# New waits, a reach for PSUM tiles, new due times and other batches in a list scheduler of a kernel of attention and two expert layers

## The chip, the cores and the metric

The kernel runs on one core of one Trainium2 chip. The metric is the device time of one execution in microseconds (us). The core's engines each work through their own list of instructions: TensorE (PE; PEld is its weight load), VectorE (DVE), ScalarE (ACT), GpSimd (POOL) and SyncE (SP), which issues the transfers.

## The reference

Attention keeps the 32 largest scores of each row (4 batches of 8 heads, 576 rows, 64 columns a head), and two gated layers follow it on 2304 rows of 512:

```python
scores = scale * np.matmul(q, k.transpose(0, 1, 3, 2))
kth = np.partition(scores, -top_k, axis=-1)[..., -top_k:-top_k + 1]
scores = np.where(scores >= kth, scores, -1e9)
attn = softmax(scores)                      # exp, divided by its sum
x = np.matmul(attn, v)                      # heads side by side: 2304 x 512
# layer 1
xn = x / np.sqrt(np.mean(x * x, -1) + 1e-6) * rms_g
g = xn @ w_gate
x = (g / (1 + np.exp(-g)) * (xn @ w_val)) @ w_out        # 512 -> 1536 -> 512
# layer 2
out = 1 / (1 + np.exp(-(x @ w_gate2))) * (x @ w_val2) @ w_out2
```

## The kernel before

The 2304 rows are 18 units of 128. For each unit VectorE takes the top 32 of eight tiles of scores (128 rows x 576, one head each): MAX8 finds eight, MATCH_REPLACE8 takes them out, four times over, and one product applies the threshold. The transposed probabilities (ph to pt, by a DMA transpose) are then multiplied by the values into pv, and the unit's rows x go into layer 1: `enter1` scales and transposes them into xt, `gate1` (gate and value product of 48 matmuls each, three times, for the three blocks of 512 columns) and `out1` (144 matmuls) make yt, and layer 2 does the same with `gate2` and `out2`. All operands are split into two float16 halves, so that each product is three.

The weights come as 64-bit numbers. `prep_piece` decodes one piece of 512 x 512 (load to raw, three steps on VectorE through a PSUM tile "dec", a matmul for the size, a scale, two float16 halves). Layer 1's nine pieces (`prep1`) stay in SBUF. Layer 2's nine pieces (`prep2`) are written to DRAM, and each batch of units loads all of them again (`load2`, 512 KB at a time) into a ring of seven buffers that raw and the halves being made use too. The first batch's loads come after the last piece (`AHEAD`, in `load2`).

Nothing is issued as it is written. A recorder (`record`, line 156) notes every operation with its engine, a planned duration (`cost`, line 185) and a due time `prio` that the program sets: TAU = 56 for a unit of attention, 7 for a tile, and for the layers a running `pos` plus a lag (line 959). The work of the layers is listed in stages (lines 946 to 962): in stage b the second layer of batch b-1 and the first layer of batch b alternate in proportion. VectorE's operations of the layers are due 160 earlier (`BIAS`).

`order` (line 212) then plays the program through. For each engine it looks at the operations whose inputs are recorded as done and whose buffers are free, takes the one that leaves the engine idle least, then the one due first; of the engines it takes the one that starts first. An operation's users may start at the time `done`, its end plus a latency by engine (260 ns for PE, 170 for VectorE, 200 for ScalarE, 150 for GpSimd) plus `MARGIN`, 120 ns. What comes out is the order of each engine's instructions and of each ring's buffers; the times on the chip follow from that order and from semaphores.

PSUM has two tiles for scores, one for pv, and three for all the rest (`ps_m`: pg, pw, py, po, dec, the small sums).

Of the kernel before, what the change touches and what calls it, by code (L numbers as in the profile page):

```python
# [16 lines left out]
PSUM = bass.MemoryType.PSUM  # L17
# [17 lines left out]
MARGIN = 120  # L35

TAU = 56.0
PREP1 = (-0.5, 0.1)  # L40
PREP2 = (0.8, 0.02)
LOADS = 0.9
LAG = (80, 1, 160)
BIAS = {"vector": 160}


BATCHES = (2,) * 9
AHEAD = 8


# [60 lines left out]


class _Op:
    __slots__ = "eng calls cost lat prio deps users waits tiles start end idx new later".split()


class _Engine:
# [7 lines left out]
class Scheduler:  # L125
# [30 lines left out]
    def record(self, eng, method, args, kw):  # L156
        writes = [x for x in (*args[:1], kw.get("out"), kw.get("accum_out")) if isinstance(x, _View)]
        reads = [x for x in (*args[1:], *(v for n, v in kw.items() if n not in ("out", "accum_out"))) if isinstance(x, _View)]
        new = not self.open
        if new:  # L160
            op = _Op()
            op.idx, op.eng, op.prio, op.calls, op.cost, op.deps, op.tiles = len(self.ops), eng, self.prio - self.bias.get(eng, 0.0), [], 0.0, set(), set()
            op.lat = 0.0
            self.ops.append(op)
            if self.open is not None:
                self.open.append(op)
        else:
            op = self.open[0]
        if self.first:
            op.deps.add(self.first)  # L170
            self.first = None
        op.calls.append((method, args, kw))
        cost, op.lat = self.cost(eng, method, args, kw, writes, reads)
        op.cost += cost
        for views, wr in ((reads, False), (writes, True)):
            for x in views:
                for other, o, w in x.tile.uses:
                    if (wr or w) and o is not op and x.overlaps(other):
                        op.deps.add(o)
        for views, wr in ((reads, False), (writes, True)):  # L180
            for x in views:
                x.tile.uses.append((x, op, wr))
                op.tiles.add(x.tile)

    def cost(self, eng, method, args, kw, writes, reads):

        out = (writes or reads)[0].shadow
        src = max([x.shadow for x in reads] + [out], key=lambda a: math.prod(a.shape[1:]))
        n = math.prod(src.shape[1:])
        psum = any(x.tile.pool.space == PSUM for x in reads + writes)  # L190
        ptrs = sum(isinstance(x, _View) for x in (*args[2:], kw.get("scalar"), kw.get("scale"), kw.get("bias")))
        if eng == "tensor":
            return math.prod(out.shape[1:]) / 2.4 + 1, 260
        if eng == "vector":
            if method in ("max", "match_replace", "tensor_tensor"):
                ptrs = 0
            fast = method in ("tensor_scalar", "tensor_copy", "memset") and not psum
            return (8 if method == "reciprocal" else 1) * n / (1.92 if fast else 0.96) + 69 + 60 * min(ptrs, 1), 170
        if eng == "scalar":
            return n * 0.8333 + (51 if psum else 93) + 93 * (ptrs + ("accum_out" in kw)), 200  # L200
        if eng == "gpsimd":
            if method == "tensor_tensor":
                return (464 if n == 1 else n * (1.88 if mybir.dt.size(out.dtype) == 2 else 2.1) + 149), 150
            return n * 0.833 + 161, 150

        run = out.shape[-1] * mybir.dt.size(out.dtype)
        size = n * math.prod(out.shape[:1]) * mybir.dt.size(out.dtype)
        if method == "dma_start_transpose":
            return 1275, size / 290
        return (475 if out.shape[0] == 128 else 650), size / (360 if run >= 512 else 180)  # L210

    def order(self):
        for op in self.ops:
            op.users, op.waits, op.start, op.end, op.new, op.later = [], len(op.deps), 0.0, None, [], []
        for op in self.ops:
            for d in op.deps:
                d.users.append(op)
        for t in self.tiles:
            for _, o, _ in t.uses[1:]:
                first = t.uses[0][1]  # L220
                if o is not first and o not in first.later and first not in o.deps:
                    first.later.append(o)
                    o.waits += 1
            t.left = len({id(o) for _, o, _ in t.uses})
            if t.uses:
                t.uses[0][1].new.append(t)
        for r in self.rings.values():
            for lane, ts in r["lanes"].items():
                r["lanes"][lane] = sorted((t for t in ts if t.uses), key=lambda t: t.uses[0][1].idx)
            r["free"] = [0.0] * r["bufs"]  # L230
        ready = {n: [] for n in self.ENGINES}
        for op in self.ops:
            if not op.waits:
                ready[op.eng].append(op)
        now = dict.fromkeys(self.ENGINES, 0.0)
        out, dma, sems, cold = [], 0.0, [0.0] * 8, COLD

        def buffers(op):
            at, seen = 0.0, {}
            for t in op.new:  # L240
                r = self.rings[t.key]
                k = seen.get(t.key, 0)
                lane = r["lanes"][t.lane]
                if t not in lane[: k + 1] or len(r["free"]) <= k:
                    return None
                at = max(at, r["free"][k])
                seen[t.key] = k + 1
            return at

        while len(out) < len(self.ops):  # L250
            best = None
            for eng in self.ENGINES:
                pick = None
                for op in ready[eng]:
                    at = buffers(op)
                    if at is None:
                        continue
                    at = max(at, op.start, now[eng])
                    if eng == "sync":
                        at = max(at, sems[0])  # L260
                        if op.calls[0][0] == "dma_start":
                            at = max(at, dma - BACKLOG)
                    key = (max(0.0, at - now[eng]), op.prio, op.idx)
                    if pick is None or key < pick[0]:
                        pick = (key, at, op)
                if pick and (best is None or pick[1] < best[1]):
                    best = pick
            if best is None:
                raise RuntimeError("the schedule is stuck")
            _, at, op = best  # L270
            cost = op.cost
            if op.eng == "tensor":

                cold = COLD if at - now[op.eng] > 2500 else cold
                slow = min(cost, cold / 2)
                cold -= 2 * slow
                cost += slow
            op.start, op.end = at, at + cost
            done = op.end + op.lat + MARGIN
            if op.eng == "sync":  # L280
                move = op.calls[0][0] == "dma_start_transpose"
                begin = max(op.end + (0 if move else 650), dma)
                dma = begin + op.lat
                done = dma + 900
                sems = sems[1:] + [done]
                if move:
                    op.end = begin + 56
            now[op.eng] = op.end
            ready[op.eng].remove(op)
            out.append(op)  # L290
            for t in op.new:
                r = self.rings[t.key]
                r["free"].pop(0)
                r["lanes"][t.lane].remove(t)
            for t in op.tiles:
                t.left -= 1
                t.end = max(t.end, done)
                if not t.left:
                    r = self.rings[t.key]
                    r["free"].append(t.end)  # L300
                    r["free"].sort()
            for u in op.users:
                u.start = max(u.start, done)
            for u in op.users + op.later:
                u.waits -= 1
                if not u.waits:
                    ready[u.eng].append(u)
        self.end = max(now.values())
        return out
# [14 lines left out]
def topk_attention_moe_kernel(  # L324
# [611 lines left out]
    state["c1"] = consts1()  # L936
    E.prio = TAU * PREP2[0]
    for j in range(NJ):
# [52 lines left out]
```

## Time and profile before

| | |
|---|---|
| time of three runs | 1275.8, 1278.83 (median), 1280.3 us |
| profiled execution | 1278.75 us, of it the span 1277.0 us |
| mean granted clock of TensorE | 0.973 |
| instructions | 41,198 |
| ScalarE and GpSimd | busy 64% of the span each |
| DMA | 215.55 MB, 169 GB/s over the span |

The span goes from the first to the last instruction. Busy time of an engine is time with an instruction in it; of TensorE the matmuls are pipelined. All operations stand at one line of the code, that of the recorder's last step, so groups go by engine, operation and tile. A clock of 1.00 is 2.4 GHz, 0.50 is 1.2 GHz, and a figure between is a mean over a stretch.

### The profile page before, as it was taken

To read this page: it belongs to the slowest core of one execution; us is meant where nothing else is said; L and a number is where in the kernel's file an instruction comes from. 1 tells how busy PE (TensorE), PEld (TensorE's weight loads), DVE (VectorE), ACT (ScalarE), POOL (GpSimd) and SP (SyncE) were. 2 spreads that over 40 slices of the span, in tenths; PEclk is the share of its full clock that TensorE was granted. 3 is DMA by queue.
4 is the path that set the end of the run, shared out by engine and by line. 5 is a ranking of instruction groups with operands and counts; after the bars stand their busy time and mean duration, and the time that the engine had idled before them with its cause. 6 is when DMAs were issued, how large, how long until landed. Compare 5 with 4: busy or idle time off the path is not lost.

```text
span 1277.0 us, 41198 instructions
## 1 busy us (share of the span) xinstructions
PE 1095.8 (86%) x16900; PEld 958.4 (75%) x16900; DVE 1037.3 (81%) x2601; ACT 811.4 (64%) x1409; POOL 814.0 (64%) x924
## 2 busy tenths in 40 slices
PE   2334465568989999999999999999999999999998
PEld 1222355558977899698879979997998898799796
DVE  6999999998978889997889889897989798880011
ACT  7995766675677666477857656775766475554321
POOL 4896786785757586486857665874858375654500
PEclk9999987679999999999999999999999999999999
DMA  8975878969578765858776694968666576844343
GB/s 277 307 208 125 236 195 237 244 176 210 127 148 190 173 143 129 184 133 168 168 185 134 121 210 121 182 156 213 143 128 149 142 164 115 192 111 125 120 133 130
DMA packets 321037, 215.55 MB, mean 169 GB/s; under 512 B 278096, under 2 KB 286288, under 8 KB 320848
## 3 DMA queue, kind: packets, MB, share of 16 engines
q1 hardware_dynamic: 320848, 212.92, 68.8%
q8 instruction: 132, 2.16, 0.7%
q14 instruction: 57, 0.47, 0.1%
HBM read 137.37 MB, written 14.16 MB: 119 GB/s over the span
## 4 chain that ended last, share of the span: by engine, by line
PE 50%; DMA 10%; DVE 6%; POOL 6%; issue 5%; ACT 4%; SPq 1%; POOLq 0%; ACTq 0%; DVEq 0%
PE pw L320 15%; PE pg L320 14%; PE po L320 8%; DMA pt<-ph 6%; PE py L320 5%; PE pv L320 3%; PE sp L320 3%; DVE m L320 3%; DVE w L320 2%; DMA xt<-sn 2%; POOL ph L320 2%; POOL sg L320 2%; DMA qt<-qn 1%; SPq L320 1%; POOL ht L320 1%
## 5 line engine op out<-in xcount | busy, mean ns | idle before, releaser
L320 DVE MAX8 m<-w 128x8 f32<-128x576 f32 x432 | 316.7, 750 | 2.9
L320 PEld LDWEIGHTS <-wl 128*128 128x128 f16 x5184 | 292.5, 98 | 3.9 <-issue 3.7
L320 POOL TENSOR_TENSOR ph<-e,ph 128x512 f16<-128x512 f32 (+1 forms) x288 | 204.5, 735 | 96.3 <-ACT ph L320 93.8
L320 DVE MATCH_REPLACE8 w<-m,w 128x576 f32<-128x576 f32 x288 | 213.1, 742 | 0.0
L320 PEld LDWEIGHTS <-w1o 128*128 128x128 f16 (+1 forms) x2640 | 153.0, 100 | 15.5 <-POOL w1o L320 11.0
L320 PE MATMUL pg<-xt,w1g 128*128 128x128 f16 x2592 | 159.4, 223 | 5.7 <-DMA xt<-sn 2.8
L320 ACT ACTIVATE e<-sp,nb,sc 128x576 f32<-128x576 f32 x144 | 116.9, 828 | 70.4 <-DVE w L320 35.1
L320 PE MATMUL pw<-xt,w1v 128*128 128x128 f16 x2592 | 155.4, 220 | 3.6 <-ACT g L320 2.0
L320 POOL TENSOR_TENSOR sg<-sg,sv 128x512 f32<-128x512 f32 x102 | 130.2, 1277 | 42.4 <-ACT sv L320 38.9
L320 PEld LDWEIGHTS <-w1g 128*128 128x128 f16 x2592 | 152.2, 100 | 6.7 <-issue 4.0
L320 PE MATMUL pg<-yt,wl 128*128 128x128 f16 x2592 | 153.8, 219 | 1.9 <-ACT sv L320 1.8
L320 PE MATMUL pw<-yt,wl 128*128 128x128 f16 x2592 | 153.5, 219 | 1.2 <-DVE ym L320 1.2
L320 PEld LDWEIGHTS <-w1v 128*128 128x128 f16 x2592 | 148.5, 99 | 4.4 <-issue 4.1
L320 PE MATMUL py<-ht,w1o 128*128 128x128 f16 x2592 | 150.3, 221 | 0.4 <-ACT sv L320 0.4
L320 DVE MAX8 m<-sp 128x8 f32<-128x576 f32 x144 | 107.8, 759 | 47.8 <-PE sp L320 47.3
L320 PE MATMUL po<-wl,ht 128*128 128x512 f16 x648 | 145.2, 379 | 0.0
L320 POOL TENSOR_TENSOR ht<-sg,ht 128x512 f16<-128x512 f32 x102 | 118.4, 1162 | 40.8 <-ACT ht L320 39.6
L320 ACT ACTIVATE ph<-e 128x576 f16<-128x576 f32 x144 | 97.5, 678 | 61.9 <-DVE e L320 58.3
L320 PE MATMUL pv<-vt,pt 128*128 128x65 f16 (+1 forms) x2240 | 93.9, 198 | 40.3 <-DMA pt<-ph 40.3
L320 PE MATMUL sp<-kt,qt 128*128 128x512 f16 (+3 forms) x640 | 98.6, 302 | 26.5 <-DVE e L320 19.0
L320 PEld LDWEIGHTS <-pt 128*128 128x128 f16 (+1 forms) x2240 | 82.6, 103 | 49.7 <-DMA pt<-ph 46.1
L320 DVE SCALAR_TENSOR_TENSOR e<-sp,m,e 128x576 f32<-128x576 f32 x144 | 115.4, 807 | 2.9
(146 smaller groups left out, 1688.5 us busy)
## 6 DMA issues: line engine op xcount, KB each, us to landing
wl<-w2g SPq DMA_DIRECT2D x54, 512.0 KB, 4.9
wl<-w2v SPq DMA_DIRECT2D x54, 512.0 KB, 4.7
wl<-w2o SPq DMA_DIRECT2D x54, 512.0 KB, 5.0
raw<-in_moe_w_gate_dram SPq DMA_DIRECT2D x24, 512.0 KB, 5.4
raw<-in_moe_w_val_dram SPq DMA_DIRECT2D x24, 512.0 KB, 4.9
raw<-in_moe_w_out_dram SPq DMA_DIRECT2D x24, 512.0 KB, 5.3
qr<-in_q_dram SPq DMA_DIRECT2D x32, 128.0 KB, 3.2
kr<-in_k_dram SPq DMA_DIRECT2D x16, 256.0 KB, 3.1
```

Source lines behind the costliest of these rows:

```text
L320: getattr(eng, method)(*map(real, a), **{n: real(x) for n, x in k.items()})
```

## The change

A wait between two dependent operations of the same engine (not of SyncE) is planned as `OWN`, 130 ns, behind the end of the first. Some planned durations are larger: a matmul by 1.7 ns, a MATCH_REPLACE by 61 ns, a small GpSimd operation by 63 ns. `order` first looks among the operations that don't open a PSUM tile or are due at most `REACH` = 100 after the earliest one left (by `base`, the due time without the bias), and among all of them only where that gives none on any engine. `PATIENCE` is 0. Layer 2's pieces are due from 0.6 TAU on in steps of 0.1 TAU (before: 0.8 and 0.02), the layers' lag begins at 95 in place of 80 (at most 160 in both), and the batches are of 1, eight times 2, and 1 unit, ten in place of nine.

```diff
--- before.py
+++ after.py
@@ -35,16 +35,22 @@
 MARGIN = 120
 
 
+REACH = 100.0
+PATIENCE = 0.0
+
+OWN = 130.0
+
+
 
 TAU = 56.0
 PREP1 = (-0.5, 0.1)
-PREP2 = (0.8, 0.02)
+PREP2 = (0.6, 0.1)
 LOADS = 0.9
-LAG = (80, 1, 160)
+LAG = (95, 1, 160)
 BIAS = {"vector": 160}
 
 
-BATCHES = (2,) * 9
+BATCHES = (1,) + (2,) * 8 + (1,)
 AHEAD = 8
 
 
@@ -111,7 +117,7 @@
 
 
 class _Op:
-    __slots__ = "eng calls cost lat prio deps users waits tiles start end idx new later".split()
+    __slots__ = "eng calls cost lat prio deps users waits tiles start end idx new later base".split()
 
 
 class _Engine:
@@ -160,7 +166,7 @@
         if new:
             op = _Op()
             op.idx, op.eng, op.prio, op.calls, op.cost, op.deps, op.tiles = len(self.ops), eng, self.prio - self.bias.get(eng, 0.0), [], 0.0, set(), set()
-            op.lat = 0.0
+            op.lat, op.base = 0.0, self.prio
             self.ops.append(op)
             if self.open is not None:
                 self.open.append(op)
@@ -190,10 +196,12 @@
         psum = any(x.tile.pool.space == PSUM for x in reads + writes)
         ptrs = sum(isinstance(x, _View) for x in (*args[2:], kw.get("scalar"), kw.get("scale"), kw.get("bias")))
         if eng == "tensor":
-            return math.prod(out.shape[1:]) / 2.4 + 1, 260
+            return math.prod(out.shape[1:]) / 2.4 + 2.7, 260
         if eng == "vector":
             if method in ("max", "match_replace", "tensor_tensor"):
                 ptrs = 0
+            if method == "match_replace":
+                return n / 0.96 + 130, 170
             fast = method in ("tensor_scalar", "tensor_copy", "memset") and not psum
             return (8 if method == "reciprocal" else 1) * n / (1.92 if fast else 0.96) + 69 + 60 * min(ptrs, 1), 170
         if eng == "scalar":
@@ -201,7 +209,7 @@
         if eng == "gpsimd":
             if method == "tensor_tensor":
                 return (464 if n == 1 else n * (1.88 if mybir.dt.size(out.dtype) == 2 else 2.1) + 149), 150
-            return n * 0.833 + 161, 150
+            return n * 0.833 + (224 if n == 1 else 161), 150
 
         run = out.shape[-1] * mybir.dt.size(out.dtype)
         size = n * math.prod(out.shape[:1]) * mybir.dt.size(out.dtype)
@@ -247,11 +255,13 @@
                 seen[t.key] = k + 1
             return at
 
-        while len(out) < len(self.ops):
+        def choose(reach):
             best = None
             for eng in self.ENGINES:
                 pick = None
                 for op in ready[eng]:
+                    if op.base > reach and any(t.pool.space == PSUM for t in op.new):
+                        continue
                     at = buffers(op)
                     if at is None:
                         continue
@@ -260,11 +270,19 @@
                         at = max(at, sems[0])
                         if op.calls[0][0] == "dma_start":
                             at = max(at, dma - BACKLOG)
-                    key = (max(0.0, at - now[eng]), op.prio, op.idx)
+                    key = (max(0.0, at - now[eng] - PATIENCE), op.prio, op.idx)
                     if pick is None or key < pick[0]:
                         pick = (key, at, op)
                 if pick and (best is None or pick[1] < best[1]):
                     best = pick
+            return best
+
+        behind = sorted(self.ops, key=lambda op: -op.base)
+        while len(out) < len(self.ops):
+
+            while behind[-1].end is not None:
+                behind.pop()
+            best = choose(behind[-1].base + REACH) or choose(math.inf)
             if best is None:
                 raise RuntimeError("the schedule is stuck")
             _, at, op = best
@@ -299,8 +317,9 @@
                     r = self.rings[t.key]
                     r["free"].append(t.end)
                     r["free"].sort()
+
             for u in op.users:
-                u.start = max(u.start, done)
+                u.start = max(u.start, op.end + OWN if u.eng == op.eng != "sync" else done)
             for u in op.users + op.later:
                 u.waits -= 1
                 if not u.waits:
```

## Rows read from the trace of the kernel before

**Rows 1.** The page, busy us (share of the span) and instructions of two engines.

```profile
PE 1095.8 (86%) x16900; PEld 958.4 (75%) x16900; DVE 1037.3 (81%) x2601; ACT 811.4 (64%) x1409; POOL 814.0 (64%) x924
```

**Rows 2.** Busy time by stage: stretch, length, engines' us (instructions), clock, DMA share, GB/s.

```profile
0.00:160.00 160.00, 60.48 (x451) 43.28 (x452) 149.25 (x381) 127.66 (x222) 116.15 (x120) 1.00 0.80 230
160.00:320.00 160.00, 106.80 (x1563) 94.92 (x1561) 151.61 (x383) 102.50 (x179) 116.82 (x129) 0.80 0.81 212
320.00:1160.00 840.00, 816.05 (x13306) 725.22 (x13304) 725.03 (x1809) 546.94 (x953) 556.95 (x657) 1.00 0.70 155
1160.00:1277.00 117.00, 112.47 (x1591) 94.95 (x1588) 11.45 (x30) 34.32 (x55) 24.13 (x20) 1.00 0.37 125
```

**Rows 3.** TensorE's waits until 320 us: us in total, times, longest us.

```profile
PE pv L320 <- DMA pt<-ph: 28.5, 16, 4.6
PE wps L320 <- DVE wh L320: 26.2, 11, 4.8
```

**Rows 4.** TensorE's waits from 320 us on, the longest in total.

```profile
PE pv L320 <- DMA pt<-ph: 11.8, 16, 1.8
```

**Rows 5.** Timeline of TensorE near the end: start us, us, operation, count.

```profile
1187.38 2.84 PE L320 MATMUL pw<-yt,wl 128*128 128x128 f16 x48
1190.06 2.84 PE L320 MATMUL pg<-xt,w1g 128*128 128x128 f16 x48
...
1200.78 15.70 PE L320 MATMUL po<-wl,ht 128*128 128x512 f16 x72
1216.32 8.20 PE L320 MATMUL py<-ht,w1o 128*128 128x128 f16 x144
```

**Rows 6.** Timeline of VectorE, two tiles interleaved, then one tile alone.

```profile
735.90 1.41 DVE L320 MAX8 m<-w 128x8 f32<-128x576 f32 x2
737.23 0.80 DVE L320 SCALAR_TENSOR_TENSOR e<-sp,m,e 128x576 f32<-128x576 f32 x1
...
755.10 0.76 DVE L320 MAX8 m<-w 128x8 f32<-128x576 f32 x1
755.90 0.09 DVE L320 MATCH_VALUE_LOAD w<-m,w 128x8 f32 x1
```

**Rows 7.** Timeline of VectorE, scales of the first and the last layer-2 piece.

```profile
134.95 0.15 DVE L320 TENSOR_SCALAR w2gs<-p2t 128x1 int32<-128x1 int32 x1
...
273.04 0.13 DVE L320 TENSOR_SCALAR w2os<-p2t 128x1 int32<-128x1 int32 x1
```

**Rows 8.** Timeline of TensorE, the first products of layer 2 and the next of layer 1.

```profile
292.74 2.84 PE L320 MATMUL pg<-yt,wl 128*128 128x128 f16 x48
...
308.27 2.84 PE L320 MATMUL pg<-xt,w1g 128*128 128x128 f16 x48
```

**Rows 9.** Busy time in two stretches while layer 2's pieces are made.

```profile
240.00:260.00 20.00, 17.64 (x267) 16.60 (x268) 19.81 (x46) 14.56 (x26) 16.64 (x18) 0.84 0.85 232
260.00:280.00 20.00, 9.69 (x142) 8.37 (x140) 20.00 (x54) 15.50 (x28) 18.60 (x20) 0.76 0.50 129
```

**Rows 10.** Groups until 700 us: xcount | busy us, mean ns | idle before, releaser.

```profile
L320 PE MATMUL pg<-xt,w1g 128*128 128x128 f16 x1296 | 82.6, 227 | 5.7 <-DMA xt<-sn 2.8 <-ACT sg L320 1.2 <-ACT g L320 0.9
...
L320 PE MATMUL pg<-yt,wl 128*128 128x128 f16 x1047 | 62.2, 219 | 1.9 <-ACT sv L320 1.8
L320 DVE MAX8 m<-sp 128x8 f32<-128x576 f32 x83 | 61.7, 757 | 23.6 <-PE sp L320 23.3
```

**Rows 11.** The page, one kind of layer-2 load: count, KB each, us to landing.

```profile
wl<-w2g SPq DMA_DIRECT2D x54, 512.0 KB, 4.9
```

**Rows 12.** Busy time and DMA during the last but one out2.

```profile
1200.00:1220.00 20.00, 20.00 (x155) 11.52 (x153) 0.00 (x0) 3.36 (x6) 4.45 (x4) 1.00 0.54 169
```

**Rows 13.** Timeline of GpSimd and ScalarE in the tail.

```profile
1229.41 1.16 POOL L320 TENSOR_TENSOR yt<-sf,yt 128x512 f16<-128x512 f32 x1 [24.14 <-ACT yt L320]
...
1273.05 0.69 ACT L320 ACTIVATE acc<-po,osc 128x512 f32<-128x512 f32 x1 [1.90 <-PE po L320]
```

## The prediction

> **What bounds the kernel now.** I read the busy shares first, then the busy time by stage, then TensorE's waits in the two halves, and last the order of single instructions. TensorE (PE) is busy 1095.8 us and VectorE (DVE) 1037.3 us [rows 1], but in different stages. Until 160 us DVE is busy 149.3 of 160 us and PE 60.5; from 160 to 320 us DVE 151.6 and PE 106.8, at a mean granted clock of 0.80; from 320 to 1160 us PE is busy 816.1 of 840 us and DVE 725.0; after 1160 us DVE has nearly nothing to do and PE is busy 112.5 of 117 us [rows 2]. So DVE sets the pace for 300 us (decoding weights and choosing the top 32), and PE from there to the end. PE idles 99.5 + 53.2 + 24.0 + 4.5 = 181 us. A gain must come from there.
>
> Early, PE waits for transposed probabilities 28.5 us and for decoded layer-2 weights 26.2 us [rows 3]; after 320 us its longest wait is 11.8 us for those probabilities, in 16 pieces [rows 4]. PE's work itself doesn't change: a product of 48 matmuls follows the next by 2.68 us, an out2 of two units takes 15.54 us [rows 5]. A unit is twelve products, an out1 of three products' length and half such an out2: 12 x 2.68 + 8.04 + 7.77 = 48.0 us, 18 times, before and after.
>
> **The change part by part.** All of it changes an order, except eighteen loads and half of the last batch's vector path.
>
> *Own waits and costs.* The old plan starts an instruction 170 + 120 = 290 ns behind an instruction of its own DVE that it needs; the new one 130 ns. The rows show both cases. Two MAX8 of different tiles and the step behind them start 1.33 / 2 = 0.665 us apart; in a tile that runs alone the load of match values starts 0.80 us behind the MAX8 that it needs [rows 6]. Dependence costs 0.135 us, so 130 ns is the size of the trace and 290 ns was not. A matmul of 128 columns is planned at 56.0 ns in place of 54.3; 2.68 us / 48 is 55.8 [rows 5]. Over 16,900 matmuls the old plan was 1.7 ns x 16,900 = 29 us short on PE.
>
> What does a truer plan give? The planner is greedy: an engine takes what can start now, and only then what waits least. With two tiles in flight the other tile's instruction can start now, so 290 or 130 ns picks the same one; only where nothing else is ready does the order change. That leaves the idle time of the middle stage, 24.0 us. Ends: a gain of all 24, or a loss where one tile runs alone more often: eight steps a tile (four MAX8, three MATCH_REPLACE, one product) x 0.135 = 1.1 us of DVE, for the 30 tiles or so until 320 us up to 32 us if none were interleaved any more. After 320 us DVE has 115 us to spare until 1160 us, which hides it. I take a gain of 4 us, a sixth of the idle time: most of it is waits on transposes that a shorter own wait doesn't shorten.
>
> The Trainium skill, "VectorE: DVE Perf Modes", section "The DRAIN you can't avoid", says that the next op does not start until the pipe is empty, and that leaving out semaphores saves nothing. By it a dependent step would cost no more than another one, the true own wait would be zero, and this part would give 0: the sum would end 4 us higher. The 0.80 beside 0.665 us speaks against it [rows 6].
>
> *No PSUM bank far behind.* An operation that opens a PSUM tile is passed over when its due time is more than 100 above the smallest that is left. How far apart are they? At 700 us DVE has scored 83 tiles, each 7 of due time: attention stands at 581. PE has done 1296 / 48 = 27 gate products of layer 1 (nine units) and 1047 / 48 = 21.8 of layer 2 (7.3 units) [rows 10]. By the lists that is the fifth stage: (4 x 48.6 + 3 x 48.0) x 56 / 48.3 = 392, plus (16.2 + 20.5) x 1.16 = 43, plus the lag of 160: 595. The two are 14 apart, so a limit of 100 doesn't bind in the steady state. I take 0. If it did bind, PE would be planned idle while it has work; that is at most a stage's lag and is in the range below.
>
> *Layer-2 weights, lag and the first batch.* Nine pieces were due at 44.8 to 53.8; now at 33.6, 39.2, ... 78.4. The first one's scale is ready at 134.95 us and the last one's at 273.04 [rows 7], 17 us a piece, and layer 2 can't start before the last is written: its first product is at 292.74, 19.7 us later [rows 8]. In these stages PE is idle 2.4 of 20 us (240 to 260) and 10.3 of 20 (260 to 280), at mean clocks of 0.84 and 0.76 [rows 9]. The pieces were all due before unit 1's tiles (56 to 105), yet unit 1 was done before the last piece; so the pieces were held by their own chain of load, decoding, matmul and write more than by due times. The first three come earlier by 11, 7 and 2, the last three later by 16 to 25. One unit alone means that layer 2 of unit 0 needs no partner, and its due times no longer alternate with unit 1's. Each us by which layer 2 starts earlier is a us of PE work moved into idle time; from 240 to 280 us there are 2.4 + 10.3 of it, so the gain ends at 13 us. The loss ends at 308.27 - 292.74 = 15.5 us: there PE goes back to layer 1 (unit 2), which was ready then. The lag rises by 15 for the first 80 of due time alone. I take a gain of 6 us, about half of the upper end, since both the first pieces and the lone unit pull that way.
>
> *One more batch.* Nine batches load 162 halves of 512 KB in all (54 of each kind), landing after a median 4.9 us [rows 11]; ten load 180. 18 x 0.524 MB = 9.44 MB. From 1200 to 1220 us the DMA engines moved 169 GB/s at a share of 0.54, so some 313 GB/s when full [rows 12]: 1.67 us a half, 30 us of DMA over the run, beside a third of its time that is free. It is on the path only in the last batch. One unit uses 18 halves in 6 x 2.68 + 7.77 = 23.9 us where DMA needs 30. Seven buffers are filled ahead; the other eleven need 18.4 us from 2.7 us on, when the first two are free, and land 3.2 us after their transfer: 24.3, for the last out2 step that begins at 21.3. That is 3 us; 0 if loads overlap better, 12 if nothing was ahead. I take 2. Behind out1 of the last unit come 1229.41 + 1.16 - 1224.36 = 6.2 us until its input for layer 2 is there (py at 1216.32 takes 8.04; [rows 5, 13]); the other batch's out2, 15.5 us, covers it, as its due point (0.8375 of the stage) lies just behind out1's (0.833). Uncovered it would cost 6. Three gates that leave the vector path go to ScalarE and GpSimd, under PE's products: 0. The end stays: last output copy at 1273.05, span 1277.0 [rows 2, 13].
>
> *Sum.* -4 + 0 - 6 + 2 = -8 us, on the profiled execution's 1278.75 us (span 1277.0 plus 1.75 around it): 1270.8 us. The median of the runs shown is 1278.83, so no correction is needed.
>
> **The rivals.** *Layer 2 starts early in full.* The start gives all 13 us and the middle 10 of its 24: 1278.75 - 13 - 10 + 2 = 1258. For it: PE's idle time from 240 to 280 us is there to be filled. Against it: DVE is full in that stage whatever the order [rows 2]. *Later pieces slip* (slower). The last four pieces, now due at 61.6 to 78.4, rank among unit 1's first four tiles, and a tile takes eight steps of 0.665 to 0.80 us, 5.3 to 6.4 us; up to 25 us of DVE can come ahead of the last piece. Layer 2 then starts at 308 or later, and PE stands without it for the 15.5 us: 1278.75 + 15.5 + 2 - 4 = 1292; half of that 1284. It decides from the point at which the last piece's scale is later than 273 + 8 us, where it eats the other gains. Against it: the pieces were not held by due times. *Nothing moves.* PE is full from 320 us and the order before is as good: -0 - 0 + 2, about 1280. *Dependence costs nothing*, the page's case: 1274.8.
>
> **How the numbers follow.** The forecast 0.42, its own range 1262 to 1276; early in full 0.18; slipping pieces 0.23; nothing moves 0.12; dependence free 0.05. The range over all is 1253 to 1289: it leaves out the far ends of the first two rivals. A measurement of this kernel tells 0.3%, 3.8 us, from no change. Faster than 1275 are nearly all of the forecast (0.39), the early case (0.18) and half of the page's case (0.03): 0.60. Same is the rest of these and "nothing moves": 0.17. Slower: 0.23.
>
> **What would show it.** In the changed kernel's profile: the last layer-2 scale before 270 us and the first product on loaded weights before 285 us (the start); PE's idle time from 320 to 1160 us down to some 20 us (the middle), with the pitch of MAX8 unchanged; 180 loads of 512 KB, and waits of PE for them only in the last 25 us, of 2 us or so. The prediction is wrong if layer 2 starts after 293 us, if PE's idle time in the middle grows, which would say that the limit of 100 binds after all, or if the last batch waits for weights by more than 5 us.

## The result, and the profile after

The changed kernel takes 1291.18 us (median of four runs, 1290.1 to 1298.58) where the kernel before takes 1279.57 on the same chip: 1.0106 times as long, 95% interval 1.0076 to 1.0136. It is slower by about 1%; the prediction said 1270.8 and faster. Its profiled execution took 1290.58 us (span 1288.7, mean granted clock 0.944) against 1278.75 (1277.0, 0.973).

First the page's busy line, then busy time by stage, with the columns of [rows 1] and [rows 2].

```profile
PE 1100.8 (85%) x16900; PEld 962.4 (75%) x16900; DVE 1042.3 (81%) x2595; ACT 815.4 (63%) x1415; POOL 822.1 (64%) x930
```

```profile
0.00:160.00 160.00, 53.91 (x389) 37.75 (x390) 148.42 (x369) 125.28 (x221) 116.39 (x117) 0.81 0.81 247
160.00:320.00 160.00, 119.38 (x1700) 103.59 (x1699) 150.68 (x376) 104.03 (x181) 114.77 (x130) 0.82 0.86 229
320.00:1160.00 840.00, 803.01 (x13101) 718.25 (x13099) 735.11 (x1824) 544.01 (x947) 554.37 (x654) 0.99 0.70 153
1160.00:1288.70 128.70, 124.46 (x1719) 102.79 (x1716) 8.11 (x28) 42.06 (x68) 36.59 (x32) 1.00 0.48 160
```

Take TensorE's idle time stage by stage: 160 - 53.91 = 106.1 (before 99.5), 40.6 (53.2), 37.0 (24.0) and 4.2 (4.5). The second stage wins 12.6 us, the middle loses 13.0 and the first 6.6. With 5.0 us more busy time for the same 16,900 matmuls that is 6.6 - 12.6 + 13.0 - 0.3 + 5.0 = 11.7 us, the difference of the spans. So in this order the first 320 us win 6.0 us of idle time in all, and the middle gives it back twice over.

The start, in VectorE's and TensorE's timelines: the scales of the first and the last layer-2 piece, and the first products of layer 2 and the next of layer 1.

```profile
119.38 0.14 DVE L339 TENSOR_SCALAR w2gs<-p2t 128x1 int32<-128x1 int32 x1
...
247.73 0.14 DVE L339 TENSOR_SCALAR w2os<-p2t 128x1 int32<-128x1 int32 x1
```

```profile
265.93 2.84 PE L339 MATMUL pg<-yt,wl 128*128 128x128 f16 x48
...
273.29 2.84 PE L339 MATMUL pg<-xt,w1g 128*128 128x128 f16 x48
```

The last scale comes 25.3 us earlier than in [rows 7], and layer 2 starts 26.8 us earlier than in [rows 8].

The middle: busy time of the changed kernel in two stretches, the first cut in 20 us, and of the kernel before over the same two.

```profile
340.00:360.00 20.00, 13.09 (x222) 11.91 (x219) 15.45 (x49) 11.36 (x23) 11.78 (x14) 0.88 0.58 95
360.00:380.00 20.00, 17.44 (x274) 16.34 (x273) 19.62 (x51) 15.47 (x29) 12.12 (x18) 0.87 0.79 144
380.00:400.00 20.00, 16.34 (x284) 15.70 (x285) 13.23 (x39) 13.99 (x26) 13.82 (x14) 0.91 0.68 136
400.00:420.00 20.00, 16.68 (x283) 15.48 (x280) 18.64 (x47) 14.35 (x26) 13.67 (x17) 0.91 0.65 118
...
860.00:980.00 120.00, 111.95 (x1794) 98.45 (x1792) 94.82 (x253) 75.58 (x134) 72.76 (x84) 0.97 0.73 155
```

```profile
340.00:420.00 80.00, 76.47 (x1183) 65.34 (x1181) 65.09 (x175) 53.19 (x96) 50.26 (x59) 0.98 0.83 186
...
860.00:980.00 120.00, 117.84 (x1961) 104.69 (x1961) 103.64 (x270) 82.95 (x147) 81.00 (x96) 1.00 0.71 160
```

From 340 to 420 us TensorE idles 80 - 63.55 = 16.5 us (before 3.5), from 860 to 980 us 8.0 (before 2.2). These two dips are 18.8 of the middle's growth; elsewhere the middle got better by 5.8. Over the 80 us of the first dip no engine is full: VectorE, the busiest, works 66.94 us, though 19.62 of 20 from 360 to 380. So I read the dip as a chain of dependent steps that runs late. This is TensorE's timeline in it (in brackets: idle time just before, and what ended it).

```profile
350.16 0.58 PE L339 MATMUL pv<-vt,pt 128*128 128x65 f16 x14
350.66 1.20 PE L339 MATMUL sp<-kt,qt 128*64 128x512 f16 x16
355.01 0.95 PE L339 MATMUL pv<-vt,pt 128*128 128x65 f16 x14 [3.14 <-DMA pt<-ph]
355.77 0.56 PE L339 MATMUL yn<-ysq,ones 128*128 128x1 f32 x2
358.87 0.37 PE L339 MATMUL pg<-yt,wl 128*128 128x128 f16 x2 [2.54 <-ACT yt L339]
360.11 5.07 PE L339 MATMUL pg<-yt,wl 128*128 128x128 f16 x46 [0.87 <-POOL yt L339]
...
405.86 4.30 PE L339 MATMUL pg<-yt,wl 128*128 128x128 f16 x45
```

TensorE waits for probabilities, then for the layer-2 input (yt) of the pair of units 1 and 2, and is then slowed: 46 matmuls take 5.07 us where 48 take 2.84. Both dips come while the next attention batch's keys and values are made. Here are their small products (tile kvt) in the changed kernel: stretch, length, TensorE's us in them (count), clock, DMA share, GB/s.

```profile
340.00:400.00 60.00, 1.94 (x12) 0.89 0.68 125
400.00:560.00 160.00, 0.00 (x0) 0.99 0.66 144
560.00:640.00 80.00, 2.56 (x16) 1.00 0.85 195
640.00:820.00 180.00, 0.00 (x0) 1.00 0.70 150
820.00:940.00 120.00, 2.73 (x16) 0.97 0.72 155
```

They are made at 340 to 400, 560 to 640 and 820 to 940 us and nowhere between; the dips lie in the first and the last of these stretches or reach into them. The stretch from 560 to 640 us has no dip (TensorE busy 77.19 of 80 us), so making them is not enough for one.

Last, attention's final step, the rows x that VectorE writes, in the changed kernel and in the kernel before (ns min/median/max, first and last start).

```profile
L339 DVE TENSOR_TENSOR x<-pv,f x32: 403/408/424, 116.6 to 1167.7; 128x256 f32<-128x256 f32 x32
```

```profile
L320 DVE TENSOR_TENSOR x<-pv,f x32: 397/412/424, 107.6 to 1158.0; 128x256 f32<-128x256 f32 x32
```

The end follows the last of them by 1288.7 - 1167.7 = 121.0 us, before by 119.0. So of the 11.7 us, 9.7 are there when attention ends.

### The profile page after: what moved, and what is told of

It reads as the page before. It is cut to its first block, busy times and chain, and to the rows that moved or that the text cites. A ratio compares the mean times of both kernels' runs of the same rounds, so it can differ in the third digit from the quotient of the medians.

```text
span 1288.7 us, 41254 instructions
## 1 busy us (share of the span) xinstructions
PE 1100.8 (85%) x16900; PEld 962.4 (75%) x16900; DVE 1042.3 (81%) x2595; ACT 815.4 (63%) x1415; POOL 822.1 (64%) x930
## 4 chain that ended last, share of the span: by engine, by line
PE 47%; DVE 17%; DMA 15%; POOL 9%; issue 6%; ACT 5%; SPq 1%; POOLq 0%; ACTq 0%; DVEq 0%
PE pw L339 14%; PE pg L339 13%; PE po L339 9%; DMA pt<-ph 8%; DVE m L339 5%; DVE w L339 5%; PE py L339 4%; POOL ph L339 3%; PE pv L339 3%; PE sp L339 3%; DMA qt<-qn 2%; DVE dec L339 2%; POOL sg L339 2%; DVE e L339 2%; POOL ht L339 1%
## 5 line engine op out<-in xcount | busy, mean ns | idle before, releaser
L339 PEld LDWEIGHTS <-wl 128*128 128x128 f16 x5184 | 298.3, 99 | 5.4 <-issue 4.3
L339 POOL TENSOR_TENSOR sg<-sg,sv 128x512 f32<-128x512 f32 x105 | 133.9, 1275 | 59.6 <-ACT sv L339 55.8
L339 PE MATMUL pg<-yt,wl 128*128 128x128 f16 x2592 | 159.9, 223 | 3.7 <-ACT yt L339 2.5
L339 POOL TENSOR_TENSOR ht<-sg,ht 128x512 f16<-128x512 f32 x105 | 121.9, 1161 | 56.7 <-ACT ht L339 52.5
L339 PE MATMUL sp<-kt,qt 128*128 128x512 f16 (+3 forms) x640 | 98.0, 301 | 33.0 <-DVE e L339 23.9
```

The source lines that it names most:

```text
L339: getattr(eng, method)(*map(real, a), **{n: real(x) for n, x in k.items()})
```

## Experiments

All ratios are against the kernel before on the same chip, with 95% intervals. "Idle" is TensorE's from 320 to 1160 us: 24.0 us before, 37.0 after the change.

### One part taken out

```diff
 undo_reach    -REACH = 100.0                +REACH = math.inf
 undo_own      -op.end + OWN if u.eng == op.eng != "sync" else done   +done
 undo_due      -PREP2 = (0.6, 0.1)           +PREP2 = (0.8, 0.02)
               -LAG = (95, 1, 160)           +LAG = (80, 1, 160)
 undo_batches  -BATCHES = (1,) + (2,) * 8 + (1,)   +BATCHES = (2,) * 9
```

> The changed kernel with REACH = infinity, all else as changed. In the changed kernel TensorE did no less work than before until 320 us and then lost 16.5 of 80 us to idle time between 340 and 420 us, where the key and value preparation of the next heads (due at 201.6) was the oldest work left. Theory 'the reach holds products back': undone, it gives that idle time back, 1278 us or less. Theory 'later pieces or lag', 'one more batch', 'own waits': within 4 us of the changed kernel's 1291. Theory 'any edit of the order scatters the time by some 10 us and no part is to blame': anything from 1275 to 1300, and the other undone parts don't add up.

> The changed kernel with the old wait of 270 to 380 ns behind an engine's own operation. Theory 'own waits' (a plan without slack: small delays on the chip make engines wait in order): 1281 us or less and fewer waits of TensorE for transposed probabilities than the 40.8 us of the changed kernel. Others: within 4 us of 1291. Theory 'scatter': anything from 1275 to 1300.

> The changed kernel with the due times of layer 2's pieces (0.8, 0.02) and the lag (80) of before. Theory 'due times': unit 1's rows come back from 242.6 to some 219 us and the time falls to 1281 us or less. Theory 'the reach': the pieces are due earlier than the last ones were, so the oldest work left moves on sooner and a part of the loss goes, 1283 to 1289. Theory 'scatter': anything from 1275 to 1300.

> The changed kernel with nine batches of two units again. Theory 'one more batch' (9.4 MB more of loads, lone units that hold a weight for one unit's work): 1281 us or less, and TensorE's idle time from 340 to 420 us gone. Theory 'the reach': within 4 us of 1291. Theory 'scatter': anything from 1275 to 1300.

| without | us | ratio | idle |
|---|---|---|---|
| reach | 1298.64 | 1.0158 (1.0113 to 1.0204) | 33.5 |
| own waits | 1308.24 | 1.0217 (1.0178 to 1.0256) | 39.0 |
| new due times and lag | 1295.69 | 1.0133 (1.0083 to 1.0184) | 38.7 |
| new batches | 1290.21 | 1.0088 (1.0055 to 1.0121) | 34.6 |

No part, taken out, gives the time of before back. Without the own waits it is slower still by 17 us; without the reach or the new due times by 7 and 4, where the intervals overlap the change's own; the batches do nothing that can be told. So none of the four parts, by itself, is the loss. What a part is worth isn't shown by this: each row is one other order, and the nanosecond runs below show how far one order lies from the next. Without the reach layer 2's first product comes at

```profile
319.12 2.84 PE L339 MATMUL pg<-yt,wl 128*128 128x128 f16 x48
```

in place of 265.93; with the old due times it comes at 273.8. That the reach is needed for an early start is not shown: a kernel below that has no part of the change, the kernel before with MARGIN = 115, starts layer 2 at

```profile
273.77 2.84 PE L320 MATMUL pg<-yt,wl 128*128 128x128 f16 x48
```

### The planned durations

```diff
 # undo_costs (in the changed kernel); before_costs does the reverse in the kernel before
-            return math.prod(out.shape[1:]) / 2.4 + 2.7, 260
+            return math.prod(out.shape[1:]) / 2.4 + 1, 260
-            if method == "match_replace":
-                return n / 0.96 + 130, 170
-            return n * 0.833 + (224 if n == 1 else 161), 150
+            return n * 0.833 + 161, 150
```

> The changed kernel with the planned durations of before (a matmul 1.7 ns shorter, MATCH_REPLACE 61 ns, a small GpSimd operation 63 ns). Theory 'longer durations are to blame': 1281 us or less. Theory 'scatter': anything from 1275 to 1305. Theory 'truer durations help': slower than the changed kernel's 1291 by 4 us or more.

> The kernel before with the larger planned durations alone. Theory 'longer durations are to blame': 8 to 20 us slower than before. Theory 'truer durations help': not slower than before. Theory 'scatter': slower than before by 5 to 30 us, as any other edit of it.

Without them the changed kernel takes 1289.34 us, 1.0094 (1.0077 to 1.0112): no difference. Alone on the kernel before they cost 1295.43, 1.0140 (1.0116 to 1.0165), with idle time of 34.2 us. The same edit, nearer to the trace [rows 5], changes nothing in one order and costs 18 us in the other. That raised the question whether the kernel before is a typical order at all.

### A nanosecond of planned wait

```diff
-MARGIN = 120
+MARGIN = 121        # 115, 119, 124 in the kernel before; 117, 121 in the changed one
```

> The kernel before with MARGIN = 121 ns in place of 120, a change of 1 ns in every planned wait that says nothing about the chip. Theory 'scatter' (the greedy plan turns any edit into another order, the order before is one of the better ones, and most others cost some per cent): clearly slower than before, by 8 us or more. Theory 'a part of the change is to blame': no more than 4 us from before.

> The kernel before with MARGIN = 119 ns. Theory 'scatter': anywhere from 2 us faster to 25 us slower than before. Theory 'a part of the change is to blame': no more than 4 us from before.

> The kernel before with MARGIN = 115 ns. Theory 'the order before was a fortunate one among its neighbours': 1290 us or more. Theory '121 ns was an unfortunate one': within 5 us of before's 1278.

> The kernel before with MARGIN = 124 ns. Theory 'the order before was a fortunate one among its neighbours': 1290 us or more, near the 1305 of 121 ns. Theory '121 ns was an unfortunate one': within 5 us of before's 1278.

> The changed kernel with MARGIN = 121 ns. Theory 'scatter' in its strong form (the changed planner's orders scatter as widely as the old one's, some 25 us for 1 ns): anything from 1275 to 1310. Theory 'the changed planner is steadier': within 6 us of the changed kernel's 1291.

> The changed kernel with MARGIN = 117 ns. Theory 'scatter': anything from 1275 to 1310. Theory 'the changed planner is steadier': within 6 us of 1291.

| kernel | MARGIN | us | ratio | idle |
|---|---|---|---|---|
| before | 115 | 1305.92 | 1.0194 (1.0171 to 1.0217) | 38.4 |
| before | 119 | 1279.05 | 1.0011 (0.9994 to 1.0027) | 24.9 |
| before | 121 | 1305.32 | 1.0205 (1.0170 to 1.0240) | 39.5 |
| before | 124 | 1303.26 | 1.0174 (1.0153 to 1.0195) | 35.6 |
| changed | 117 | 1291.27 | 1.0080 (1.0062 to 1.0098) | 31.1 |
| changed | 121 | 1292.08 | 1.0081 (1.0061 to 1.0102) | 31.6 |

One nanosecond of planned wait, which changes none of the engines' work and no true duration, costs the kernel before some 26 us. So a loss of this size needs no part of the change. These two rows are of the kernel before with 121: the page, and the middle stage.

```profile
PE 1109.0 (85%) x16900; PEld 970.3 (74%) x16900; DVE 1036.2 (79%) x2601; ACT 810.6 (62%) x1409; POOL 813.0 (62%) x924
320.00:1160.00 840.00, 800.52 (x12720) 707.51 (x12718) 713.61 (x1792) 529.66 (x926) 537.08 (x639) 0.98 0.69 152
```

This execution's span is 1308.1 us, 31.1 longer than before. Of it 15.5 us are idle time in the middle (39.5 in place of 24.0) and 13.2 are TensorE's busy time, 1109.0 us for the same matmuls where the kernel before has 1095.8.

Is 1279 or 1305 the exception? The sequence of the matmuls in the traces, compared by tile, helps here. With 119 all 16,900 come in the order of 120, so it is the same draw twice. With 115, 121 and 124 only 8,464 to 9,926 stand at the place that they have with 120, and these three orders, all that differ, lie at 1303 to 1306. The order before is a fortunate one among its neighbours. But the three are not three independent draws: each two of them agree at 13,035 to 15,128 places.

The changed kernel lies at 1291 to 1292 at 117, 120 and 121, which are three different orders. Against the three slow neighbours the change is a gain of some 13 us; against the one order it was measured with, a loss of 12; against the mean of the four orders of the kernel before, 1298.5 us, a gain of 7. Four and three orders are too few to say what the change is worth.

Nor is the changed kernel's early gain the same in each of its orders. With 117 its first two stages are

```profile
0.00:160.00 160.00, 53.58 (x390) 37.22 (x391) 150.19 (x370) 125.82 (x221) 116.79 (x118) 0.59 0.83 247
160.00:320.00 160.00, 110.82 (x1668) 100.13 (x1667) 149.66 (x374) 103.85 (x180) 114.40 (x128) 0.80 0.81 219
```

so TensorE idles 155.6 us until 320 us, and 156.2 with 121, where the kernel before idles 152.7 and the change as measured 146.7. Yet layer 2 starts at 269.56 and 270.29 in them, nearly as early as 265.93.

The neighbour's loss looks like the change's: dips, in other places. The longest of before with 121:

```profile
640.00:660.00 20.00, 17.52 (x253) 16.70 (x250) 12.23 (x34) 14.42 (x28) 12.61 (x15) 0.83 0.68 147
660.00:680.00 20.00, 16.58 (x253) 15.19 (x250) 16.19 (x47) 11.94 (x23) 13.13 (x17) 0.91 0.41 85
680.00:700.00 20.00, 16.70 (x257) 15.81 (x258) 19.34 (x56) 13.90 (x25) 10.46 (x14) 0.83 0.58 116
```

### The reach without the key and value work

```diff
-        behind = sorted(self.ops, key=lambda op: -op.base)
+        held = ("kr", "ks", "kt", "vr", "vt", "kvn", "kvt", "p2tkv")
+        behind = sorted((op for op in self.ops if not all((t.key[1] in held or t.args[2].startswith("kv"))
+                         for t in op.tiles)), key=lambda op: -op.base)
```

> The changed kernel, with the preparation of keys and values (tiles kr, ks, kt, vr, vt and their scales) left out of the list whose smallest due time the reach starts from. Theory 'the stall at 340 to 420 us comes from the reach, held at 201.6 by the next heads' preparation that waits for buffers': TensorE's idle time from 340 to 420 us falls from 16.5 to under 8 us, and the time to 1285 or less if no other stretch pays for it. Theory 'a stretch with few tiles ready starves TensorE in most orders': the idle time stays within 5 us of 16.5 or turns up elsewhere, and the time stays within 5 us of 1291.

1289.97 us, 1.0091 (1.0056 to 1.0126). From 340 to 420 us 12.0 us are idle in place of 16.5. Holding the reach for keys and values has a hand in the dip at most, and nothing that can be told in the time.

### Other constants for the changed planner

These are constants with which the planner's own end comes early, picked from a few thousand.

```diff
 # searched_margin142; searched_margin143 differs by MARGIN = 143
-MARGIN = 120    -REACH = 100.0   -OWN = 130.0
+MARGIN = 142    +REACH = 123.0   +OWN = 80.0
-PREP1 = (-0.5, 0.1)  -PREP2 = (0.6, 0.1)   -LOADS = 0.9
+PREP1 = (-0.7, 0.1)  +PREP2 = (0.6, 0.08)  +LOADS = 0.7
-LAG = (95, 1, 160)   -BIAS = {"vector": 160}
+LAG = (105, 1, 141)  +BIAS = {"vector": 98}
-BATCHES = (1,) + (2,) * 8 + (1,)
+BATCHES = (1, 1) + (2,) * 8
 # searched_margin63: BACKLOG 6692, MARGIN 63, REACH 120, OWN 100, TAU 57, PREP1 (-0.38, 0.1),
 # PREP2 (0.47, 0.14), LAG (90, 1, 165), BIAS 148, the same batches
```

> The changed planner with MARGIN 142, OWN 80, REACH 123, lag 105 to 141, key loads due later, bias 98, one unit alone in the first two batches: shortest plan with a margin of 108 ns or more. Theory 'a search over orders finds better ones than before's': 1279 us or less, and nearer to its plan than with 63 ns. Theory 'before's order can't be beaten this way': 1283 us or more.

> The same with MARGIN = 143 ns, the neighbour. Theory 'the changed planner is steadier': within 4 us of 142 ns. Theory 'scatter': up to 25 us slower.

> The changed planner with other constants (MARGIN 63, OWN 100, REACH 120, due times, lag 90 to 165, one unit alone in the first two batches, TAU 57), the one whose plan was shortest of a few thousand. Theory 'the order is what matters and a search over orders finds better ones than before's': 1279 us or less. Theory 'a plan with small waits is late on the chip': 1285 us or more.

142: 1279.75 us, 0.9994 (0.9972 to 1.0016), idle 27.2. 143: 1278.50, 0.9994 (0.9969 to 1.0019), idle 23.9. 63: 1287.65, 1.0066 (1.0046 to 1.0087). The changed planner can equal the kernel before, but none of these beats it. That 142 and 143 agree says nothing of steadiness: all 16,900 matmuls come in the same sequence in both. With 142 the dip is gone:

```profile
340.00:420.00 80.00, 75.22 (x1276) 66.98 (x1274) 71.25 (x196) 59.10 (x110) 56.75 (x66) 1.00 0.96 208
```

### What makes the dip at 340 us: the pairing of units 1 and 2?

In the changed kernel SyncE issues no layer-2 load between 318.38 and 366.81 us (load, us of issue, count), three more until 375.09 and then none until 416.89. The first goes out once the product that had waited for the pair's input (at 360.11) is done; I take it that until then the ring's buffers are held.

```profile
366.81 0.53 SPq L339 DMA_DIRECT2D wl<-w2v  x1
372.58 1.05 SPq L339 DMA_DIRECT2D wl<-w2g  x2
375.09 0.57 SPq L339 DMA_DIRECT2D wl<-w2v  x1
416.89 0.35 SPq L339 DMA_DIRECT2D wl<-w2v  x1
```

The two sets of constants were crossed with the two ways to batch unit 1. (The lists also differ at the end: where unit 1 is in a pair, the last unit is alone.)

```diff
 # after_two_alone, in the changed kernel
-BATCHES = (1,) + (2,) * 8 + (1,)
+BATCHES = (1, 1) + (2,) * 8
 # searched_pairs, in searched_margin142: the reverse
```

> The changed kernel with units 0 and 1 in batches of their own (1, 1, and eight times 2) and none alone at the end. In the changed kernel four of the seven weight buffers stand full from about 335 to 365 us, because layer 2 of the pair of units 1 and 2 has to wait for unit 2's input, and TensorE idles 16.5 us from 340 to 420 us. Theory A (that stall comes from the pairing): the transfers of layer-2 halves go on between 335 and 365 us, the idle time from 340 to 420 us falls to about 5 us, and the time to about 1281 if nothing is given back later. Theory B (each order has its own dips; a cure in one place moves them elsewhere): the idle time from 340 to 420 us falls too, but that of 320 to 1160 us stays above 30 us, and the time between 1285 and 1297. Theory C (the stall there has another cause): the idle time from 340 to 420 us stays above 12 us.

> The constants of searched_margin142 with the change's own batches (1, eight times 2, 1). The fourth cell of a table: changed constants or searched ones, unit 1 in a pair or alone. Theory A (the pairing makes the stall): TensorE idles some 12 us or more from 340 to 420 us, where it idled 4.8 with unit 1 alone, and the time is about 1289, some 9 above searched_margin142. Theory B (the batches are one roll of the dice among others): idle time from 340 to 420 us of 5 to 17 us, with the time between 1280 and 1295 and no tie between the two. If it ends below 1276, it is faster than both kernels, and the search has found what neither predicts.

| | unit 1 paired with 2 | unit 1 alone |
|---|---|---|
| constants of the change | 1291.18, 1.0106 | 1296.46, 1.0130 (1.0094 to 1.0167) |
| constants of 142 | 1287.50, 1.0067 (1.0047 to 1.0087) | 1279.75, 0.9994 |

With the other constants the pairing brings a like picture back: a wait for probabilities, shorter waits for layer 2's input than in the change (0.39 us in place of 2.54), some half of the idle time (80 - 70.45 = 9.5 us from 340 to 420; theory A asked for 12), and some 8 us of time. The middle as a whole idles 37.4 us in place of 27.2, so half of its growth lies elsewhere.

```profile
351.09 0.95 PE L339 MATMUL pv<-vt,pt 128*128 128x65 f16 x14 [3.89 <-DMA pt<-ph]
351.85 0.56 PE L339 MATMUL kvt<-kvn,ones 128*128 128x1 f32 x2
352.80 0.37 PE L339 MATMUL pg<-yt,wl 128*128 128x128 f16 x2 [0.39 <-ACT yt L339]
354.04 5.06 PE L339 MATMUL pg<-yt,wl 128*128 128x128 f16 x46 [0.87 <-POOL yt L339]
```

But in the changed kernel, taking the pairing away doesn't help. Loads do go on (four from 344.44 us on, one at 361.93), TensorE is busy 18.31 of 20 us from 340 on, and the next 20 us are the worst of all, with 11.51 busy; 13.7 us are idle in the 80, 39.6 in the middle. Now the waits are for keys and values (TensorE from 340 to 420 us: what it waited for, us, times, longest):

```profile
PE kvt L339 <- ACT vt L339: 3.3, 2, 1.9
PE pg L339 <- DMA xt<-sn: 2.9, 1, 2.9
PE kvt L339 <- ACT ks L339: 2.0, 2, 1.3
```

The changed kernel's neighbours, with MARGIN 117 and 121, tell more. They have the same pair, and these are their 80 us:

```profile
340.00:420.00 80.00, 73.23 (x1239) 66.49 (x1237) 70.80 (x191) 57.95 (x103) 53.17 (x63) 0.94 0.82 176
340.00:420.00 80.00, 73.06 (x1255) 68.42 (x1253) 64.68 (x179) 58.35 (x106) 56.04 (x63) 0.96 0.64 135
```

They idle 6.8 and 6.9 us there in place of 16.5 (with 121 no layer-2 load is issued between 353.17 and 395.19 us either), and take 1291 and 1292 us all the same; undo_batches, with 5.1 us there, takes 1290. So the pair alone doesn't make that stall, and the dip at 340 us is not what the time hangs on: without it the time is lost elsewhere. What decides how deep an order's dips get stays open. Several of them lie where the next keys and values are made, but not all: with 121 the kernel before idles 5.0 us from 540 to 560 us, where none of their products are made. No run tests whether keys and values are a cause.

## Why the prediction was wrong, step by step

*What bounds the kernel.* Right as a map of stages: VectorE until 320 us, TensorE from there. What it didn't say is that the 24.0 us of idle time in the middle [rows 2] were, beside the neighbours' 35.6 to 39.5, a low number already.

*Own waits and costs, -4.* This is the step that failed. It is the only term for the middle's idle time, and it took the order before as a typical order, from which truer waits could only take idle time away or do nothing; it bounded the loss by tiles that run alone until 320 us. The idle time from 320 to 1160 us rose from 24.0 to 37.0 instead. Three neighbours of the kernel before, with no part of the change, have 35.6 to 39.5: an edit that moved the order could land there whatever it was meant to do. "Where nothing else is ready does the order change" was true of one choice, but each choice that differs moves all that follow. The size of the own wait stands (0.135 us, [rows 6]), but what planning it gives isn't shown: without it the changed kernel takes 1308.24 us, without the new durations 1289.34, one order each. It isn't a term of its own that can be added.

From the Trainium skill, "VectorE: DVE Perf Modes", section "The DRAIN you can't avoid", I read that a dependent step costs no more than another, by which this part was to give 0. I read it too widely. The same section of the Trainium skill also says that a next op that is not held starts earlier. The trace agrees: interleaved steps start 0.665 us apart, closer than the 0.76 us that one MAX8 takes [rows 6]. What that makes of the time the runs don't decide: an order that plans the own wait differently is another order, and that outweighs the wait.

*PSUM reach, 0.* I looked at the steady state alone. At the start the reach does change the order: without it layer 2 comes at 319 us in place of 266, and the kernel takes 1298.64 us, one order. The test I named, idle time in the middle that grows because the limit binds, can't tell: without the reach the middle still idles 33.5 us, and the neighbours without any part of the change idle more.

*Layer-2 weights and first batch, -6.* The signs came: the last scale at 247.73 and layer 2 at 265.93, both beyond what I asked for (270 and 285). The step from there to the gain, that each us by which layer 2 starts earlier is a us of work moved into idle time, doesn't hold. The stage from 160 to 320 us won 12.6 us and the first 160 lost 6.6, in all 6.0, which is the number forecast, but by luck: layer 2 came 26.8 us earlier for it, and at MARGIN 117 some 23 us earlier, with 2.9 us more idle time until 320 us than before. From 240 to 280 us, where I had counted 13 us to be won, it won 4.7 (12.7 to 8.0). The rival "later pieces slip" is refuted, though its time, 1284 to 1292, held: the loss has another place.

*One more batch, +2.* 180 loads as said, and TensorE waits for them 0.3 us, in one wait before the last gate product of the last unit:

```profile
1272.00 2.52 PE L339 MATMUL pg<-yt,wl 128*128 128x128 f16 x42 [0.26 <-DMA wl<-w2g]
```

*The sum.* By stages: first 160 us +6.6 and the next 160 us -12.6 (-6 for both), middle +13.0 (-4), last stage -0.3 (+2), and 5.0 of busy time that no step had: "PE's work itself doesn't change" was right of the 16,900 matmuls and wrong of the time that they take, since TensorE is granted half its clock behind some of its waits (0.50 from 360 to 365 us, below).

## What to carry to other kernels

Before an edit of a list scheduler is priced from the trace of one order, run that order's neighbours: change a planned wait by a nanosecond and see what the time does. See, too, whether the neighbour's sequence is another at all: with 119 and with 143 it was not. If the time moves by 2%, as here, a tuned kernel may be a fortunate draw, an edit may draw anew, and a part's worth is the difference between two groups of neighbours, not between two kernels. Then look for what the draws have in common (here: 111 to 127 us from attention's last rows to the end, and dips that often lie where keys and values are made). An edit there might help every one of them; that was not tried.

## What the runs showed of the hardware

A short starvation of TensorE was paid twice here. In the changed kernel it waits 3.14 and 2.54 us within 9 us and does only short products between; the 46 matmuls that follow take 5.07 us against 46/48 of 2.84 = 2.72 at 2.4 GHz. The granted clock while they run is 0.50, that is 1.2 GHz:

```profile
360.00:365.00 5.00, 4.89 (x46) 4.80 (x45) 4.95 (x10) 2.79 (x6) 1.58 (x4) 0.50 0.09 17
```

Four stretches of 20 us in a row show mean granted clocks of 0.87 to 0.91, and further waits, of up to 3.5 us, follow in them. In all the same matmuls cost 5.0 us more than before, beside 6.7 us more of waiting; in the kernel before with MARGIN = 121 they cost 13.2 more.
